# Half of a weight block loaded later, and the last two shuffles of an inverse transform sent by halves on three queues

## The chip, the cores and the metric

The kernel runs on one core of a Trainium2 chip. The metric is the device time of one execution in microseconds. A core has TensorE (matmul), VectorE, ScalarE, GpSimd and SyncE, which run their own instruction streams and wait for each other through semaphores, and 16 DMA engines, which move data on behalf of whichever engine issued the transfer. In the profile these are PE (with PEld for its weight loads), DVE, ACT, POOL and SP.

## The reference

S = 2048 positions, D = 448 channels, a hidden size F = 1792, everything in bf16. With LN a layer norm over D without weights:

```
h   = q + LN(q) * y,   y = causal convolution over S of kv with ssm_k, plus kv * ssm_D
kv  = v * (4-tap causal convolution of k with shift_k)
h2  = h + transpose( gelu( LN(LN(h))^T @ w1 + b1 ) @ w2 + b2 )
```

The long convolution is written as rfft, product, irfft of length 2 S. The MLP mixes positions: w1 is S x F, w2 is F x S.

## The kernel before, in words

The positions are split as s = 16 q + r: q is the partition (128 of them) and r the row (R = 16). A transform of length 4096 is done in two stages of matmuls, with a shuffle of partitions between them, which is a DMA from SBUF to SBUF. So there is a forward stage 1 for the filter and for kv (`emit_stage1`, tables E), its shuffles (L947), a forward stage 2 (`emit_stage2`, L964), and then the way back in `emit_products_i1`: for each of eight pairs jj the complex products on VectorE (L1015), inverse stage 1 on TensorE (L1027), the evacuation of PSUM into the SBUF tile TU (L1031, which is the helper `evac`: its instructions carry lines 652 and 653 on ScalarE and 655 and 656 on VectorE), and the shuffle of TU into the tile TZ (L1037). TU is indexed [partition, j, h, d] with j = 0 to 15 and h = 0, 1 the two halves of a complex number. An evacuation of pair jj writes one h for both j = 2 jj and 2 jj + 1. A shuffle moves one j with both h: 112 partitions of it from GpSimd's queue, 16 partitions from SyncE's.

Inverse stage 2 (`emit_i2`, L1104) is two matmuls for each of the 16 rows. It reads, for every row, all 16 shuffles, so it starts only once the last has landed. Behind it per row come the gate on ScalarE or VectorE (L1111), a combination on VectorE (L1118), the second layer norm (sums on ScalarE L1134, small steps on GpSimd L1141 to L1153, the normalised row Q on VectorE L1159), and, interleaved on TensorE, the first seven blocks of the MLP's first layer (L1203), which use the weights W1A. The other seven blocks (L1213) use W1B, the second layer (L1223) uses W2. The results go out at L1231 and L1234.

Between inverse stages 1 and 2 there are filler matmuls (`emit_warm`, L1047): 34 of them (N_WZ) ahead of stage 2, and 6 and 8 more inside it. They compute nothing that is used. The statistics of q for the first layer norm are on VectorE (L1069, L1071) with two small steps on GpSimd for each group of two rows (L1074, L1077), in whatever gaps there are.

The loads: q into X (L838) and W1A in four parts of four rows each (L1178) wait for the last shuffle of kv (`shuf["upool15"]`). W2 (L1188, four parts) and W1B (L1181, four parts) wait for the last large inverse shuffle (`shuf["zpool"]`). All of them are issued by SyncE (WQ), whose instruction stream is in order, as every engine's is. TK and TU give their space to W2, V and the tables E give theirs to W1B.

The order of instructions isn't written out by hand. `op(...)` records each operation with what it reads and writes, and when all are recorded a planner (`schedule`) walks through simulated time. When an engine comes free, it takes the ready operation with the earliest due time `sch.t0` (the length of the path behind it only breaks near ties), using estimated durations and one shared rate for DMA. `emit` then writes the instructions in the planned order and adds the waits. Due times that matter here: 7.01 + 0.974 i for the inverse products, evacuations and shuffles (i = 15 gives 21.62), T_Q = 83.98 and later for the statistics of q, 35.76 and later for the 34 fillers, 85.76 and later for stage 2, T_W1 = 122.45 for W1A, T_W1 + 4 = 126.45 for W2, T_WB = 154.44 for W1B.

Of the kernel before, what the change touches and what calls it, by code (L numbers as in the profile page):

```python
# [98 lines left out]
class _Sched:  # L99
# [48 lines left out]
    def op(self, W, fn, r=(), w=(), br=(), bw=(), n=0, kind=None, est=None, dmab=None, keng=16, rate=None, after=(), safter=()):  # L148
        o = _Op()
        o.id = len(self.ops)  # L150
        o.engs = W if isinstance(W, tuple) else (W,)
        o.eng = None
        o.fn = fn
        o.is_dma = dmab is not None
        o.nbytes = dmab or 0
        o.keng = keng
        o.lat = 2000.0 + o.nbytes / (22.0 * keng) if o.is_dma else 70.0
        if o.is_dma:
            o.est = {e: (600.0 if e != "pool" else 820.0) for e in o.engs}
        elif est is not None:  # L160
            o.est = dict(est) if isinstance(est, dict) else {e: est for e in o.engs}
        else:
            o.est = {e: self.est_of(e, n, kind) for e in o.engs}
        o.ev = None
        o.t0 = self.t0
        o.rate = rate or (18.0 if keng == 8 else 26.0)
        o.tag = self.tag
        o.acq = []
        o.bufs = []
        o.extra = []  # L170
        preds = set(after)
        spreds = set(safter)
        for spec in r:
            for c in self._cells(spec):
                preds.update(c.w)
                c.r.append(o.id)
        for spec in w:
            g = spec[2] if len(spec) > 2 else None
            for c in self._cells(spec):
                rd = [x for x in c.r if x != o.id]  # L180
                if g is not None and c.g == g and not rd:
                    preds.update(c.gb)
                    c.w.append(o.id)
                else:
                    base = rd if rd else list(c.w)
                    preds.update(base)
                    c.w = [o.id]
                    c.r = []
                    c.g = g
                    c.gb = base  # L190
        for b in br:
            if len(self.ops) and all(self.ops[x].engs == ("pe",) for x in b.writers):
                preds.add(b.writers[-1])
            else:
                preds.update(b.writers)
            b.readers.append(o.id)
            o.bufs.append(b)
            b.users.append(o.id)
        for b in bw:
            if not b.writers:  # L200
                o.acq.append(b)
            else:
                spreds.add(b.writers[-1])
            b.writers.append(o.id)
            o.bufs.append(b)
            b.users.append(o.id)
        preds.discard(o.id)
        spreds -= preds
        o.preds = sorted(preds)
        o.spreds = sorted(spreds)  # L210
        self.ops.append(o)
        return o.id
# [297 lines left out]
def _build(nc, A_q, A_k, A_v, A_shift_k, A_ssm_k, A_ssm_D, B_w1, B_b1, B_w2, B_b2, out):  # L510
# [8 lines left out]
    R = 16  # L519
    NFC = F // 128  # L520
    EPS = 1e-5
    DB = 2 * D
# [15 lines left out]
    o_W1A = 0  # L538
# [8 lines left out]
    o_TU = 104064  # L547
    o_KN = o_TU
    o_W2 = (o_TK, o_TU)
    o_TZ = 132736  # L550
# [15 lines left out]
    with ctx:  # L566
        sch = _Sched(nc, ctx, n_dma_sems=112, small_off=SMALL)
        op = sch.op
# [4 lines left out]
        def view(off, shape, dtype=bf16):  # L573
            size = 4 if dtype in (f32, i32) else 2
            n = 1
            for s_ in shape:
                n *= s_
            ap = AR[:, off // 2: off // 2 + n * size // 2]
            if dtype is not bf16:
                ap = ap.bitcast(dtype)  # L580
            if len(shape) == 2:
                ap = ap.rearrange("p (a b) -> p a b", b=shape[1])
            elif len(shape) == 3:
                ap = ap.rearrange("p (a b c) -> p a b c", b=shape[1], c=shape[2])
            return ap
# [8 lines left out]
        TU = view(o_TU, [R, 2, D])  # L594
        KN = view(o_KN, [4, S])
        W2 = [view(o, [NFC // 2, S]) for o in o_W2]
        TZ = view(o_TZ, [R, 2, D])
# [15 lines left out]
        def MR(s):  # L613
            return view(o_WR + s * 4 * DB, [4, D])
# [13 lines left out]
        def Pb(b, i=0):  # L628
            return PS[:, b.slots[i], 0:D]

        def Ppair(b):
            s0, s1 = b.slots
            return PS[:, s0:s1 + 1, 0:D]
# [7 lines left out]
        T_Q, T_DQ, T_I2, T_DI2, T_M1, T_W1 = 83.98, 14.35, 85.76, 0.401, 102.98, 122.45  # L641

        T_TH, T_TN = -36.0, -30.0
        T_CP, T_XL, T_WB = 20.0, -35.53, 154.44
# [309 lines left out]
        shuf = {}  # L954
# [50 lines left out]
        def emit_products_i1():  # L1005
            for jj in range(R // 2):
                ms = []
                for h in range(2):
                    i = 2 * jj + h
                    sch.t0 = T_I1 + T_DI1 * i  # L1010
                    m = _Buf(mring)
                    ms.append(m)
                    ru = (o_TU + i * 2 * DB, 2 * DB)
                    aft = [x for w in wbufs for x in w.readers] if i == 0 else [mfirst[0]]
                    op("dve", lambda e, W, m=m, i=i: e.tensor_tensor(  # L1015
                        out=MR(m.slots[0]).rearrange("p (x y) d -> p x y d", x=2),
                        in0=TU[:, i].unsqueeze(2).broadcast_to([128, 2, 2, D]),
                        in1=TK[:, i].unsqueeze(1).broadcast_to([128, 2, 2, D]), op=ALU.mult),
                       r=[ru, (o_TK + i * 2 * DB, 2 * DB)], bw=[m], n=4 * D, after=aft)
                    if i == 0:  # L1020
                        mfirst.append(len(sch.ops) - 1)
                bs = [_Buf(psum, 2) for _ in range(2)]
                for h in range(2):
                    for t, (tab, xy) in enumerate(((MA, 0), (MN, 3), (MB, 1), (MB, 2))):
                        for par in range(2):
                            P = slice(64 * par, 64 * par + 64)
                            k = op("pe", lambda e, W, b=bs[h], m=ms[h], par=par, t=t, tab=tab, xy=xy, P=P: e.matmul(  # L1027
                                Pb(b, par), tab[P, :], MR(m.slots[0])[P, xy, :], start=(t == 0), stop=(t == 3)),
                               r=r_iv, br=[ms[h]], bw=[bs[h]], n=D, est=D / 4.15)
                            i1_last.append(k)  # L1030
                    evac(lambda jj=jj, h=h: TU[:, 2 * jj:2 * jj + 2, h, :], lambda b=bs[h]: Ppair(b),  # L1031
                         [(o_TU + (4 * jj + h) * DB, DB), (o_TU + (4 * jj + 2 + h) * DB, DB)], bs[h], 2 * D)
                for par in range(2):
                    j = 2 * jj + par
                    p0 = 64 * (j & 1) + 32 * ((j >> 1) & 1) + (j >> 2)
                    for q_, a, b_, j0 in (("pool", 0, 112, 0), ("sp", 112, 128, 14)):
                        shuf["z" + q_ + str(j)] = shuf["z" + q_] = op(q_, lambda e, W, j=j, p0=p0, a=a, b_=b_, j0=j0: e.dma_start(  # L1037
                            TZ[p0:p0 + 29:4, j0:j0 + (b_ - a) // 8].rearrange("p r c d -> p r (c d)"),
                            TU[a:b_, j].rearrange("p c d -> p (c d)")),
                           r=[(o_TU + j * 2 * DB, 2 * DB)], w=[(o_TZ + j0 * 2 * DB, (b_ - a) // 8 * 2 * DB, "z" + q_)],  # L1040
                           dmab=(b_ - a) * 2 * DB, keng=8)
# [130 lines left out]

        def emit_w1_load(which):
            for h in range(4):
                sch.t0 = (T_W1, T_WB)[which] + 0.1 * h * (1 - which)
                rs = slice(4 * h, 4 * h + 4)
                if which == 0:
                    op(WQ, lambda e, W, rs=rs: e.dma_start(W1A[:, rs, :], w1d[:, rs, 0:896]),  # L1178
                       w=[(o_W1A + 4 * h * 1792, 4 * 1792)], dmab=128 * 4 * 1792, after=[shuf["upool15"]])
                else:  # L1180
                    op(WQ, lambda e, W, rs=rs: e.dma_start(W1B[:, rs, :], w1d[:, rs, 896:1792]),  # L1181
                       w=[(o_W1B + 4 * h * 1792, 4 * 1792)], dmab=128 * 4 * 1792, after=[shuf["zpool"]])
# [100 lines left out]
```

## Time and profile before

| | |
|---|---|
| median of five runs | 189.56 us (188.29 to 191.54) |
| the profiled execution's own time | 189.56 us |
| its span in the profile | 187.7 us |
| TensorE busy | 174.2 us (93%) |
| VectorE, ScalarE, GpSimd busy | 109.9, 97.3, 70.9 us |
| TensorE's granted clock | 1.00 |
| moved by DMA | 35.43 MB, 129 GB/s of HBM traffic over the span |

The 1.86 us between the time and the span lie around the span. The profile has a page with each engine's busy time, groups of instructions by source line, and a chain of waits: followed back from the last instruction, at each step, to what released it. A timeline lists the instructions of an engine in order of time, equal neighbours merged, with the idle time before them and what ended it. A table of windows gives the busy time of every engine in a stretch. A DMA's duration on its issuing engine is only the issue; the landing is counted from the start of the issue to the end of the transfer.

### The profile page before, as it was taken

What the parts mean: (1) busy time and instruction counts of PE and PEld (TensorE: products, weight loads), DVE (VectorE), ACT (ScalarE), POOL (GpSimd) and SP (SyncE); (2) the same over time, 40 slices, a digit from 0 to 9 for tenths busy, and PEclk for the clock granted to TensorE, in tenths of its full rate; (3) what the DMA queues carried; (4) which work ended last, traced back from release to release, by engine and by line L of the source; (5) the groups of instructions that cost most, each with busy time, mean ns of one, the idle gap of its engine ahead of it and who ended that gap; (6) DMA issues with size and microseconds to landing.
All of it is one profiled execution on the core that took longest, in us unless ns stands there. A gap on an engine that the chain in (4) does not pass through costs nothing.

```text
span 187.7 us, 2824 instructions
## 1 busy us (share of the span) xinstructions
PE 174.2 (93%) x1033; PEld 91.6 (49%) x1033; DVE 109.9 (59%) x181; ACT 97.3 (52%) x141; POOL 70.9 (38%) x176
## 2 busy tenths in 40 slices
PE   7998898988988989899989999999999999999993
PEld 2752343423432433244435545555557777777771
DVE  8877999777789999997879756000001122222221
ACT  3597989788789989950986483442121000000000
POOL 8936977678520034577178566000000000000000
PEclk9999999999999999999999999999999999999999
DMA  5997688787449997773999999000000110111111
GB/s 160 413 416 287 187 242 237 213 250 220 119 120 376 391 377 215 226 228 116 320 421 418 419 402 369 10 0 0 0 0 3 49 43 6 49 52 49 49 49 49
DMA packets 15724, 35.43 MB, mean 189 GB/s; under 512 B 3869, under 2 KB 9886, under 8 KB 15710
## 3 DMA queue, kind: packets, MB, share of 16 engines
q1 hardware_dynamic: 11102, 25.59, 36.3%
q0 software_dynamic: 4608, 9.66, 17.8%
q8 instruction: 8, 0.13, 0.3%
q14 instruction: 6, 0.05, 0.1%
HBM read 22.37 MB, written 1.84 MB: 129 GB/s over the span
## 4 chain that ended last, share of the span: by engine, by line
PE 68%; DMA 9%; ACT 8%; DVE 5%; POOL 5%; issue 3%; ACTq 0%; SPq 0%; POOLq 0%
PE ps L1223 23%; PE ps L1213 11%; PE ps L1203 10%; DMA arena<-arena 9%; PE ps L1027 5%; ACT arena L652 4%; PE ps L964 4%; PE ps L1104 3%; POOL arena L947 3%; PE ps L914 3%; PE ps L904 3%; ACT arena L943 2%; PE ps L1047 2%; ACT arena L1111 1%; PE ps L996 1%
## 5 line engine op out<-in xcount | busy, mean ns | idle before, releaser
L1227 DVE SCALAR_TENSOR_TENSOR arena<-ps,arena 128x448 bf16<-128x448 f32 x16 | 10.9, 684 | 56.9 <-PE ps L1223 56.9
L1223 PE MATMUL ps<-arena 128*128 128x448 bf16 x224 | 42.5, 352 | 0.0
L1223 PEld LDWEIGHTS ps<-arena 128*128 128x128 bf16 x224 | 32.3, 144 | 10.1
L943 ACT CAST arena<-ps 128x896 bf16<-128x896 f32 x32 | 26.8, 928 | 4.1 <-PE ps L933 1.5
L652 ACT CAST arena<-ps 128x896 bf16<-128x896 f32 (+1 forms) x26 | 22.0, 909 | 2.6 <-PE ps L868 1.6
L1203 PE MATMUL ps<-arena 128*128 128x448 bf16 x112 | 23.0, 353 | 0.3 <-DVE arena L1159 0.2
L947 POOL DMA_DIRECT2D arena<-arena x32 | 19.2, 601 | 8.5 <-ACT arena L943 5.0
L1213 PE MATMUL ps<-arena 128*128 128x448 bf16 x112 | 21.4, 352 | 0.0
L1193 ACT ACTIVATE arena<-ps,arena 128x448 bf16<-128x448 f32 x14 | 8.2, 639 | 20.1 <-PE ps L1213 14.7
L964 PE MATMUL ps<-arena 128*64 128x448 bf16 x128 | 16.4, 362 | 2.0 <-ACT arena L652 1.0
L879 DVE TENSOR_TENSOR arena<-arena 128x1792 bf16<-128x1792 bf16 x16 | 18.2, 1173 | 0.0
L1111 ACT ACTIVATE arena<-ps,arena 128x448 f32<-128x448 f32 x16 | 11.2, 721 | 12.3 <-PE ps L1104 9.3
L1037 POOL DMA_DIRECT2D arena<-arena x16 | 9.4, 594 | 20.8 <-PE ps L964 15.6
L933 PE MATMUL ps<-arena 128*128 128x448 bf16 x64 | 16.0, 355 | 1.3 <-ACT arena L943 1.3
L885 PE MATMUL ps<-arena 128*128 128x448 bf16 x64 | 14.5, 353 | 2.4 <-ACT arena L943 1.9
L1015 DVE TENSOR_TENSOR arena<-arena 128x1792 bf16<-128x1792 bf16 x16 | 16.4, 1084 | 0.0
L1203 PEld LDWEIGHTS ps<-arena 128*128 128x128 bf16 x112 | 10.9, 98 | 11.1 <-DVE arena L1159 1.3
L1213 PEld LDWEIGHTS ps<-arena 128*128 128x128 bf16 x112 | 11.0, 98 | 10.2
L1027 PE MATMUL ps<-arena 64*128 64x448 bf16 x128 | 14.1, 351 | 1.3 <-DVE arena L1015 0.6
L1118 DVE SCALAR_TENSOR_TENSOR arena<-arena 128x448 f32<-128x448 bf16 x16 | 10.7, 676 | 4.8 <-ACT arena L1111 4.8
L964 PEld LDWEIGHTS ps<-arena 128*64 128x64 f16 x128 | 5.4, 108 | 11.7 <-ACT arena L652 4.6
L655 DVE CAST arena<-ps 128x896 bf16<-128x896 f32 (+2 forms) x11 | 9.5, 877 | 2.7 <-PE ps L868 1.2
(87 smaller groups left out, 197.9 us busy)
## 6 DMA issues: line engine op xcount, KB each, us to landing
arena<-arena POOLq DMA_DIRECT2D x48, 196.0 KB, 4.9
arena<-in_B_w_dram SPq DMA_DIRECT2D x8, 896.0 KB, 12.9
arena<-in_B_w_dram SPq DMA_DIRECT2D x2, 2048.0 KB, 10.4
arena<-in_B_w_dram SPq DMA_DIRECT2D x2, 1536.0 KB, 17.5
arena<-in_A_k_dram SPq DMA_DIRECT2D x4, 448.0 KB, 7.4
arena<-in_A_v_dram SPq DMA_DIRECT2D x4, 448.0 KB, 8.0
arena<-in_A_q_dram SPq DMA_DIRECT2D x4, 448.0 KB, 4.6
out_dram<-arena SPq DMA_DIRECT2D x7, 224.0 KB, 1.9
```

What stands on the lines that cost most here:

```text
L652: return e.copy(out=dst(), in_=src())
L879: op("dve", lambda e, W, T=T, i=i, r=r: e.tensor_tensor(out=T[:, i], in0=KH[:, r:r + 4, :], in1=WT, op=ALU.mult), r=[(o_KH + r * DB, 4 * D ...
L885: op("pe", lambda e, W, b=b, T=T, i=i, j=j: e.matmul(Pb(b, i), ID, T[:, i, j, :], start=(j == 0), stop=(j == 3)), r=[(o_ID, 256), (o + (i ...
L933: op("pe", lambda e, W, b=b, r=r, h=h, dl=dl: e.matmul(Pb(b, h), E[:, 2 * r + h, :], src[:, r, :], start=True, stop=not dl), r=[r_E(r), (o ...
L943: return e.copy(out=dst, in_=Ppair(b)) if W == "act" else e.tensor_copy(out=dst, in_=Ppair(b))
L947: shuf[tag + q_ + str(r)] = shuf[tag + q_] = op(q_, lambda e, W, w=w, p0=p0, a=a, b_=b_, j0=j0: e.dma_start(T[p0:p0 + 29:4, j0:j0 + (b_ - ...
L964: op("pe", lambda e, W, b=bs[h], h=h, j=j, c=c, par=par: e.matmul(PS[64 * par:64 * par + 64, b.slots[c], 0:D], FW[:, 64 * c:64 * c + 64], ...
L1015: op("dve", lambda e, W, m=m, i=i: e.tensor_tensor(out=MR(m.slots[0]).rearrange("p (x y) d -> p x y d", x=2), in0=TU[:, i].unsqueeze(2).br ...
L1027: k = op("pe", lambda e, W, b=bs[h], m=ms[h], par=par, t=t, tab=tab, xy=xy, P=P: e.matmul(Pb(b, par), tab[P, :], MR(m.slots[0])[P, xy, :], ...
L1203: op("pe", lambda e, W, r=r, fc=fc, b=bs[fc]: e.matmul(Pb(b), W1A[:, r, 128 * fc:128 * fc + 128], Q[:, r, :], start=(r == 0), stop=(r == R ...
L1213: op("pe", lambda e, W, r=r, fc=fc, b=b: e.matmul(Pb(b), W1B[:, r, 128 * (fc - n0):128 * (fc - n0) + 128], Q[:, r, :], start=(r == 0), sto ...
L1223: op("pe", lambda e, W, r=r, fc=fc, b=b: e.matmul(Pb(b), W2[fc // 7][:, fc % 7, r:S:R], G[:, fc, :], start=(fc == 0), stop=(fc == NFC - 1) ...
```

## The change

The change has two parts.

First, for the last pair of inverse shuffles (jj = 7, j = 14 and 15) the two h are sent apart, so that each transfer depends on one evacuation only. The h = 0 halves go as before: 112 partitions from GpSimd, 16 from SyncE. Of the h = 1 halves, the 112 partitions of j = 14 go from GpSimd and those of j = 15 from SyncE, and both times the 16 remaining partitions from ScalarE's queue. `shuf["zpool"]` is then the transfer of j = 15, h = 1 on SyncE.

Second, parts 2 and 3 of W1A (rows 8 to 15) wait for `zpool` instead of `upool15`, with a due time 30 earlier (92.45). W1B's due time is 30 earlier as well (124.44), which puts it ahead of W2 (126.45).

```diff
@@ emit_products_i1, in the loop over jj, ahead of the shuffles
+                if jj == R // 2 - 1:
+                    for h in range(2):
+                        for par in range(2):
+                            j = 2 * jj + par
+                            p0 = 64 * (j & 1) + 32 * ((j >> 1) & 1) + (j >> 2)
+                            o_h = o_TU + (2 * j + h) * DB
+                            for q_, a, b_, j0 in (("sp" if h and par else "pool", 0, 112, 0), ("act" if h else "sp", 112, 128, 14)):
+                                k = op(q_, lambda e, W, j=j, h=h, p0=p0, a=a, b_=b_, j0=j0: e.dma_start(
+                                    TZ[p0:p0 + 29:4, j0:j0 + (b_ - a) // 8, h, :], TU[a:b_, j, h, :]),
+                                       r=[(o_h, DB)], w=[(o_TZ + j0 * 2 * DB, (b_ - a) // 8 * 2 * DB, "zpool" if a == 0 else "zsp")],
+                                       dmab=(b_ - a) * DB, keng=8)
+                                if a == 0:
+                                    shuf["zpool"] = k
+                    continue
@@ emit_w1_load
-                sch.t0 = (T_W1, T_WB)[which] + 0.1 * h * (1 - which)
+                sch.t0 = (T_W1 - 30.0 * (h > 1), T_WB - 30.0)[which] + 0.1 * h * (1 - which)
...
-                       w=[(o_W1A + 4 * h * 1792, 4 * 1792)], dmab=128 * 4 * 1792, after=[shuf["upool15"]])
+                       w=[(o_W1A + 4 * h * 1792, 4 * 1792)], dmab=128 * 4 * 1792,
+                       after=[shuf["upool15" if h < 2 else "zpool"]])
```

## The prediction

> **What bounds the kernel now.** I read the chain of waits first, then the timeline of TensorE, GpSimd and ScalarE around the place that the change touches, then the windows of the stages behind it. The chain, in order of time (start us, us, what), from the last inverse products on:
>
> ```profile
> 79.59 0.91 ACT arena L652
> 80.50 0.28 issue
> 80.79 1.17 POOL arena L1037 x2
> 81.95 0.07 issue
> 82.03 0.24 POOL arena L1074
> ...
> 82.35 0.72 POOL arena L1077
> 83.07 0.64 POOL arena L1037
> 83.71 4.62 DMA arena<-arena
> 88.33 0.05 issue
> 88.37 1.70 PE ps L1104 x8
> ```
>
> So the last shuffle of TU into TZ (L1037) starts at 83.71, lands at 88.33, and the inverse stage 2 (L1104) starts at 88.37. It reads as if every microsecond off that shuffle were a microsecond off the kernel. TensorE's timeline (start, busy us, line, count, idle before) says otherwise:
>
> ```profile
> 81.62 6.60 PE L1047 MATMUL ps<-arena 128*128 128x448 f16 x34
> 88.37 1.69 PE L1104 MATMUL ps<-arena 128*128 128x448 bf16 x8
> ```
>
> The 34 filler matmuls of L1047 stand in TensorE's program ahead of L1104. A matmul lasts 352 ns and overlaps the next, so 6.60 us = 33 steps + 0.352, a step of 0.189 us. The last filler starts at 81.62 + 6.25 = 87.87 and the next matmul could start at 88.06. TensorE therefore waits for the shuffle for only 88.37 - 88.06 = 0.31 us. The weight loads say the same within their own lead: 0.59 us idle, put down to the DMA.
>
> Behind that point TensorE is the bound (us, then busy time and count of PE, PEld, DVE, ACT, POOL; clock; DMA share; GB/s):
>
> ```profile
> 88.37:112.80 24.43, 23.21 (x116) 10.46 (x116) 18.60 (x56) 17.86 (x40) 14.25 (x37) 1.00 0.97 383
> 112.80:120.94 8.14, 8.12 (x43) 4.22 (x44) 2.86 (x7) 2.50 (x8) 3.04 (x8) 1.00 0.55 209
> 120.94:142.13 21.19, 21.19 (x114) 11.05 (x112) 0.00 (x0) 6.49 (x12) 0.00 (x0) 1.00 0.00 0
> ```
>
> From 88.37 to the end there are about 1.2 us in which TensorE does not work. All else is a fixed count of matmuls, 14 more fillers among them, at a granted clock of 1.00.
>
> **The last pair of shuffles.** Before, j = 14 and 15 need both evacuations of the pair, and are 2 issues on GpSimd (587 to 674 ns) and 2 small ones on SyncE (0.67 us). GpSimd:
>
> ```profile
> 80.79 1.17 POOL L1037 DMA_DIRECT2D arena<-arena  x2 [0.84 <-ACT arena L652]
> 82.03 0.24 POOL L1074 TENSOR_SCALAR arena<-arena 128x2 f32<-128x2 f32 x1
> 82.35 0.72 POOL L1077 TENSOR_TENSOR arena<-arena 128x2 f32<-128x2 f32 x1
> 83.03 1.27 POOL L1037 DMA_DIRECT2D arena<-arena  x2
> ```
>
> ScalarE's timeline has the two last evacuations back to back:
>
> ```profile
> 80.65 1.85 ACT L652 CAST arena<-ps 128x896 bf16<-128x896 f32 x2 [0.15 <-PE ps L1027]
> 88.96 2.57 ACT L1111 ACTIVATE arena<-ps,arena 128x448 f32<-128x448 f32 x4 [6.46 <-PE ps L1104]
> ```
>
> so half h = 0 is ready at about 81.57 and h = 1 at 82.50. After, there are 8 issues: 3 on GpSimd, 3 on SyncE, 2 on ScalarE. GpSimd is free at 81.96; its two h = 0 halves take it to 81.98 + 2 x 0.59 = 83.16, and the third (j = 14, h = 1) starts there: 0.55 us before the last one of now. The statistics steps L1074/L1077 fall behind all three, because their due time (83.98) is later than the shuffles' (21.62) and the planner now has a shuffle ready for each free slot. SyncE is free at 81.9 (its jj = 6 issues began at 80.52 and take 0.67 each); two small ones, then the large j = 15, h = 1 starts at 81.93 + 2 x 0.67 = 83.27. ScalarE issues its two small ones from 82.53.
>
> Landings. On GpSimd the shuffles of this stage land 3.7 to 6.0 us after issue starts, median 4.8; the last took 4.62. Half the bytes in the same number of rows: at best 3.7, at worst 6.0; I take the last one's own 4.62, giving 83.16 + 4.62 = 87.78. The Trainium skill (DMA: Bandwidth & Descriptors, section Anatomy of one DMA — SWDGE (gpsimd) path) puts a transfer at a fixed part of about 2.0 us plus bytes over 436 GB/s. By it halving 196 KB saves an estimated 0.23 us, and a half is through some 2.2 us after its 0.59 us issue, at 86.0. The trace is twice as slow, and I use the trace; the sum is the same by both, since both fall ahead of 88.06. The same page (section Issuing engines are not separate DMA queues) speaks against the split: more issuing engines save only issue time, because all run on the same 16 DMA engines. By that rule the gain is the 0.55 us of issue above, not a shorter flight.
>
> No SyncE shuffle of this size stands in the trace. Nearest below are its output stores, 112 KB in 1.7 us; nearest above its X loads, 448 KB in 3.6 to 5.8 us under a full DMA. I take 3.7, the fastest GpSimd shuffle, since it too is SBUF to SBUF: 87.0, with ends 85.0 and 89.1. A DMA from ScalarE is not in the trace at all. Its issue is bounded by 0.59 (GpSimd's) and 1.30 us (SyncE's longest at L1037), an addition, so no gain; I take 0.67 each. They hide in ScalarE's 6.46 us idle before L1111 at 88.96, which is what is queued behind them; with that cover gone they would cost 1.3 us. Their landing has the bounds of the SyncE ones, and a first use of a queue gives a third row: SyncE's very first load, 256 KB, landed in 3.7. From 83.2 that is 86.9. What a third queue costs outside the span lies between 0 and 0.9 us (two queues and everything else fit in 189.56 - 187.7 = 1.86); no row separates it out, so I take 0 and keep the end for the range.
>
> So all of TZ is there at about 87.8, and L1104 starts at 88.06 instead of 88.37: **-0.31 us**. The other 0.28 us of earlier landing goes into the fillers. Next to be late is TensorE itself. Four more semaphore waits ahead of L1104 count as nothing: after the last landing all the remaining ones took 0.04 us.
>
> **GpSimd behind it.** One more issue (0.59) pushes the last statistics step before stage 2 from 88.03 to 88.6. The gate of row 0 needs only the first step, done at about 84.8; rows 8 and 9 need the last one at 97. GpSimd's next other work is at 92.47. Nothing.
>
> **The moved loads.** Two of four W1A loads (2 x 896 KB) leave the stretch 56 to 70. There the DMA is full (share 1.05 at 64 to 68), but the chain from 55 to 80 has no DMA in it, and shuffles issued under that load land in 4.4 to 5.1 us, not later than those after it. Gain: nothing. They reappear behind the SyncE half, ahead of W1B and W2, with the due times putting W1B before W2. Before, W2 and W1B are 10752 KB = 11.0 MB, at 413 GB/s 26.7 us, from about 90.3 to 117. After, SyncE resumes at about 87.0, data flows from about 89, and the half W1A takes 1.84 MB / 413 = 4.4 us, to 93.5; W1B 8.9 us, to 102.4; W2 17.8 us, to 120. Add 1 us for completion. Needs: W1A's row 8 is matmul 57 of L1203, the sixth of the seven that start at 107.61, hence 108.6; W1B at 120.94; W2 at 142.13. Margins 14, 17 and 21 us. If the old order W2 before W1B had been kept, W1B would land at 121 and its first matmul wait; it isn't. SyncE has no other work until the stores at 148.18. Starting these loads while the last GpSimd half is in flight costs nothing by the row just quoted.
>
> **The order.** The planner is list scheduling over the whole program, so an edit may reorder far away. By its own costs the fillers (34 at 190 ns, from the last product on) end 0.1 us after the last shuffle already before, so stage 2 starts at the same planned time in both, and the loads needed later are there long before. I expect the same order on TensorE, VectorE and ScalarE.
>
> Sum against the profiled execution: span 187.7 - 0.31 = 187.4; time 189.56 - 0.31 = 189.25. That execution's time equals the median of the runs, so **189.3**.
>
> **Rivals.** (a) *The landing sets the start.* If the planner put fewer fillers ahead of L1104, or the halves' short landing pulled more than 0.31 us: landing at 87.0 to 87.8 gives 0.6 to 1.4 us, 188.2 to 189.0. For it: the chain names the shuffle. Against it: the fillers' count, and TensorE's 1.2 us of idle behind, which caps even a better order. Chance 0.07.
> (b) *Slower: the last quarter lands late.* Place: ScalarE's second small shuffle, begun at 83.2, or SyncE's large one, begun at 83.27, ahead of L1104. It decides from a landing of 88.33, that is 5.1 us of flight; each microsecond beyond is one lost. At the slowest flight in this stage, 6.0 us, it lands at 89.3: +0.9, 190.5. For it: rows of 896 B instead of 1792 B, and a queue never used in the trace. Against: 3.7 for a first use. Chance 0.10.
> (c) *It doesn't do what it says.* L1074 and L1077 (1.04 us with gaps) still fall ahead of the last GpSimd half, as they do now: start 84.2, landing 88.8, +0.45: 190.0. For it: they do so in the profile. Against: the due times. Chance 0.05.
>
> **How the numbers follow.** The forecast, 189.3, has 0.78. The five runs spread from 188.29 to 191.54, and about 1% is what a measurement of this kernel can tell from no change. The range reaches down to rival (a) and up past (b): 188.3 to 190.7. Faster by over 1% needs 1.9 us, more than the idle that is there: 0.05. Slower by over 1% needs a flight of 7 us or a reordered stage 2: 0.10. Within 1%: 0.85.
>
> **What would show it.** Right: the fillers still x34 and ending near 88.2, L1104 starting at about 88.1 with no wait for the DMA, three GpSimd issues in a row before L1074, W1A's halves landing before 95, no wait for a load in L1203 or L1213. Wrong: L1104 still waiting for a DMA beyond 88.4; another interleaving of L1104, L1047 and L1203; matmuls of L1203 waiting on a load near 108.

## The result, and the profile after

The changed kernel takes 190.11 us (median of 43 executions, 187.83 to 193.31) beside 189.84 us for the kernel before (80 executions, 187.40 to 192.70). The ratio is 1.0025, with a 95% interval from 1.0006 to 1.0044: slower by about 0.5 us, with 0.1 and 0.8 as the ends. That ratio counts only executions within 1.5% of the fastest of their own kernel; over all of them the means differ by 0.38 us, with an interval from -0.1 to 0.9 (95%, by resampling the listed times). So how much slower it is, and whether it is at all, is less sure than the first interval looks, but a gain of 0.31 us, which was the forecast, lies outside both. The time itself lies inside the range and within the 1% that was called no change, but the sign was wrong.

The profiled execution of the changed kernel has a span of 186.9 us, 0.8 less than the one of before, and that says nothing about the change. Its fillers start at 80.90 instead of 81.62, because loads and shuffles ahead of 50 us, which the change doesn't touch, happened to come earlier. So the stretches have to be compared one by one. The chain of the changed kernel (start us, us, what) around the place of the change:

```profile
80.87 0.91 ACT arena L652
81.79 0.14 SPq L1040
81.92 0.04 issue
81.97 1.33 SPq L1040
83.30 0.04 issue
83.34 4.49 DMA arena<-arena
87.83 0.09 issue
87.92 1.69 PE ps L1118 x8
```

Before, the last piece ahead of stage 2 was GpSimd's second shuffle (4.62 us from 83.71). Now it is a SyncE one, the large half of j = 15, which starts 1.56 us behind the last evacuation (83.34 against 81.78) and flies 4.49 us. SyncE goes on with W1A at 87.85, which confirms the landing, since that load waits for this half. TensorE's timeline:

```profile
80.90 6.61 PE L1061 MATMUL ps<-arena 128*128 128x448 f16 x34
87.92 1.67 PE L1118 MATMUL ps<-arena 128*128 128x448 bf16 x8 [0.42 <-DMA arena<-arena]
```

From the first filler to stage 2 it is 7.02 us, against 6.75 before and 6.44 if nothing but the 34 fillers counted. The wait for the DMA did not go; between these two profiles it grew by 0.27 us. GpSimd and ScalarE did what the prediction had written down for them, apart from ScalarE's two issues, which took 1.96 us instead of 1.34:

```profile
81.22 1.75 POOL L1040 DMA_DIRECT2D arena<-arena  x3
83.05 0.42 POOL L1088 TENSOR_SCALAR arena<-arena 128x2 f32<-128x2 f32 x2
...
81.81 1.96 ACTq L1040 DMA_DIRECT2D arena<-arena  x2
```

Behind stage 2 the two profiles agree window by window (columns as in the prediction):

```profile
87.92:112.36 24.44, 23.20 (x117) 10.45 (x117) 18.63 (x56) 17.89 (x40) 14.26 (x37) 1.00 0.99 377
112.36:120.48 8.12, 8.12 (x43) 4.22 (x44) 2.83 (x7) 2.48 (x8) 3.03 (x7) 1.00 1.03 418
120.48:141.67 21.19, 21.19 (x113) 11.05 (x112) 0.00 (x0) 6.48 (x12) 0.00 (x0) 1.00 0.04 15
```

These are 24.44, 8.12 and 21.19 us against 24.43, 8.14 and 21.19. The DMA is full some 4 us longer (share 1.03 in the second window instead of 0.55), and TensorE doesn't notice.

### The profile page after: what moved, and what is told of

It is laid out like the page before. It is cut to its first block, busy times and chain, and to the rows that moved or that the text cites. A ratio compares the mean times of both kernels' runs of the same rounds, so it can differ in the third digit from the quotient of the medians.

```text
span 186.9 us, 2835 instructions
## 1 busy us (share of the span) xinstructions
PE 174.2 (93%) x1033; PEld 91.6 (49%) x1033; DVE 110.0 (59%) x181; ACT 97.1 (52%) x141; POOL 72.1 (39%) x177
## 4 chain that ended last, share of the span: by engine, by line
PE 72%; DMA 10%; ACT 8%; DVE 6%; issue 2%; SPq 1%; ACTq 0%
PE ps L1238 23%; PE ps L1228 11%; PE ps L1218 10%; DMA arena<-arena 7%; PE ps L885 5%; PE ps L1027 5%; ACT arena L652 4%; PE ps L964 4%; PE ps L1118 3%; PE ps L933 3%; DMA arena<-in_A_ssm_k_dram 3%; DVE arena L1015 2%; PE ps L914 2%; ACT arena L943 2%; PE ps L1061 2%
## 5 line engine op out<-in xcount | busy, mean ns | idle before, releaser
L1218 PE MATMUL ps<-arena 128*128 128x448 bf16 x112 | 23.0, 353 | 0.3 <-DVE arena L1173 0.2
L947 POOL DMA_DIRECT2D arena<-arena x32 | 19.2, 601 | 6.5 <-ACT arena L943 3.5
L1228 PE MATMUL ps<-arena 128*128 128x448 bf16 x112 | 21.4, 352 | 0.0
L964 PE MATMUL ps<-arena 128*64 128x448 bf16 x128 | 16.4, 362 | 1.8 <-ACT arena L652 1.0
L1218 PEld LDWEIGHTS ps<-arena 128*128 128x128 bf16 x112 | 10.9, 98 | 11.1 <-DVE arena L1173 1.3
L1051 POOL DMA_DIRECT2D arena<-arena x14 | 8.2, 588 | 20.8 <-PE ps L964 15.6
L1228 PEld LDWEIGHTS ps<-arena 128*128 128x128 bf16 x112 | 11.0, 98 | 10.2
L964 PEld LDWEIGHTS ps<-arena 128*64 128x64 f16 x128 | 5.4, 108 | 11.4 <-ACT arena L652 4.6
```

What stands on the lines that cost most here:

```text
L947: shuf[tag + q_ + str(r)] = shuf[tag + q_] = op(q_, lambda e, W, w=w, p0=p0, a=a, b_=b_, j0=j0: e.dma_start(T[p0:p0 + 29:4, j0:j0 + (b_ - ...
L964: op("pe", lambda e, W, b=bs[h], h=h, j=j, c=c, par=par: e.matmul(PS[64 * par:64 * par + 64, b.slots[c], 0:D], FW[:, 64 * c:64 * c + 64], ...
L1218: op("pe", lambda e, W, r=r, fc=fc, b=bs[fc]: e.matmul(Pb(b), W1A[:, r, 128 * fc:128 * fc + 128], Q[:, r, :], start=(r == 0), stop=(r == R ...
L1228: op("pe", lambda e, W, r=r, fc=fc, b=b: e.matmul(Pb(b), W1B[:, r, 128 * (fc - n0):128 * (fc - n0) + 128], Q[:, r, :], start=(r == 0), sto ...
```

## The experiments

The times of whole executions scatter by 1 to 2% for causes ahead of the change, so the main measure is the stretch F, from the start of the first filler to the start of stage 2. From stage 2 to the end of the last VectorE instruction it was 96.83 to 96.86 us in every profile at full clock in that stretch, of every kernel below. F is therefore where the kernels differ behind the fillers.

| kernel | F in each profile, us | time against before, 95% interval |
|---|---|---|
| before | 6.75, 7.04, 6.91 | |
| changed | 7.02, 6.99, 7.20 | 1.0025 (1.0006 to 1.0044) |
| shuffles only | 7.12 | 1.0009 (0.9976 to 1.0042) |
| loads only | 6.44, 6.53, 7.09 | 0.9997 (0.9946 to 1.0049) |
| changed, small ones on SyncE | 7.18 | 1.0017 (0.9969 to 1.0065) |
| changed, all large halves on GpSimd | 6.66, 6.62, 6.70 | 1.0108 (1.0048 to 1.0168), then 0.9990 (0.9955 to 1.0026) |
| the same without the moved loads | 7.16 | 0.9966 (0.9934 to 0.9997) |
| whole rows from ScalarE and SyncE | 6.69 (at a clock of 0.94), 7.98 | 1.0004 (0.9972 to 1.0036) |
| loads only, statistics behind, 31 fillers | 6.87 | 0.9971 (0.9940 to 1.0002) |
| before, one shuffle more | 7.76 | |
| before, half the bytes in the last pair | 6.44 | |

### One part at a time

The first part alone is the changed kernel with the load function of before; the second alone is the kernel before with

```diff
-                sch.t0 = (T_W1, T_WB)[which] + 0.1 * h * (1 - which)
+                sch.t0 = (T_W1 - 30.0 * (h > 1), T_WB - 30.0)[which] + 0.1 * h * (1 - which)
...
-                       after=[shuf["upool15"]])
+                       after=[shuf["upool15" if h < 2 else "zpool"]])
```

> The first part of the change alone: the last pair of shuffles by halves on three queues; all of W1A waits for the kv shuffles and W2 goes before W1B, as before. Measure: from the start of the first of the 34 fillers to the start of inverse stage 2, which is 6.75 us before and 7.02 after the change, with 6.44 the floor that the fillers set. Theory (the SyncE half of j = 15 starts late, because the ScalarE and SyncE issues slow each other, and flies long): 7.0 us, the same as with the whole change, and a time 0.2 to 0.4 us above before. Rival (the moved loads cost it): 6.75 or less, and no slower than before.

> The second part alone: half of W1A and all of W1B wait behind the last shuffle, W2 last; the shuffles as before. Theory (late SyncE half): fillers to stage 2 stay at 6.75 us, from stage 2 to the end 96.2 us as in both profiles, time within 0.2% of before. Rival (the loads cost it): a longer stretch behind stage 2, or 7.0 us ahead of it, and a time 0.2 to 0.4% above before.

Shuffles only: F = 7.12, as with the whole change. Loads only: no wait at all in the first profile.

```profile
80.31 6.61 PE L1047 MATMUL ps<-arena 128*128 128x448 f16 x34
86.75 1.49 PE L1104 MATMUL ps<-arena 128*128 128x448 bf16 x7
```

So the lateness seems to come with the split, not with the loads, on one profile each. The times are too blunt to say it: both intervals hold 1. What was not expected is that F fell to the floor with the loads moved. The stretch was profiled twice more.

> The moved loads alone, once more, for a second profile. If moving W1A out of the stretch before really speeds the last shuffle, stage 2 is at the floor of 6.44 us behind the first filler again. If the 6.44 was one draw of a scattering landing, it is 6.7 to 7.0 as in the profiles of before.

> The moved loads alone, a third profile. If moving half of W1A speeds the last shuffle, 6.44 to 6.6 us from the first filler to stage 2; if the two low ones were chance, 6.75 or more.

It gave 6.53 and then 7.09, with a wait again:

```profile
83.21 6.61 PE L1047 MATMUL ps<-arena 128*128 128x448 f16 x34
90.30 0.55 PE L1104 MATMUL ps<-arena 128*128 128x448 bf16 x2 [0.48 <-DMA arena<-arena]
```

Whether the moved loads help the landing stays open on these three. Behind stage 2 they cost nothing, as the unchanged stretch shows.

### How much F scatters

The kernel before and the changed one were run unchanged.

> The kernel before, unchanged, for a second profile of the same stretch. If the stretch from the first of the 34 fillers to stage 2 is a property of the kernel, it is 6.75 us again, within 0.1; if landings of the last shuffle scatter, it can be anything from the floor of 6.44 to 6.9.

> The changed kernel, unchanged, for a second profile. Theory (the hardware-queue half of j = 15 lands last): 6.9 to 7.2 us again, and the shuffle that lands last is SyncE's, since SyncE goes on with W1A in the same tenth of a microsecond as stage 2 starts. Rival (scatter): below 6.75.

> The kernel before, a third profile. From the first filler to stage 2 it had 6.75 and 7.04. If it belongs between the moved loads alone (6.44, 6.53) and the changed kernel (7.02, 6.99, 7.20), it has 6.7 to 7.05 again. If all three are one scatter, it can be 6.44 or 7.2.

> The changed kernel, a third profile. 7.0 us from the first filler to stage 2 again if the lateness is the kernel's; scatter would show as 6.7 or less.

Before has 6.75, 7.04, 6.91 (mean 6.90), changed 7.02, 6.99, 7.20 (mean 7.07). The second profile of before:

```profile
83.35 6.61 PE L1047 MATMUL ps<-arena 128*128 128x448 f16 x34
90.39 0.55 PE L1104 MATMUL ps<-arena 128*128 128x448 bf16 x2 [0.43 <-DMA arena<-arena]
```

The landing scatters by some 0.3 us in the same program. The wait of 0.31 us that the prediction was built on was one draw; over three profiles it is 6.90 - 6.44 = 0.46. The means differ by 0.17 us, which lies inside the measured 0.1 to 0.8 us, but the two sets overlap: 7.04 of before is above 7.02 and 6.99 of the changed kernel. Where the rest of the middle value (0.47) would be was not found, and with these scatters it need not exist.

### ScalarE's issues, taken away

```diff
-("act" if h else "sp", 112, 128, 14)
+("sp", 112, 128, 14)
```

> The whole change, but the two small h = 1 shuffles go from SyncE's queue behind its large one, and ScalarE issues none. Theory (the issues of ScalarE and SyncE slow each other): SyncE's second small issue takes 0.7 us instead of 1.33, its large half starts 0.6 us earlier and lands 0.5 us earlier, at some 6.4 to 6.6 us behind the first filler; stage 2 starts at 6.45 to 6.6 us, time 0.3 to 0.5 us below that of the whole change. Rival (flight alone is long, the engines' bandwidth ends it): the large half still lands at about 6.9 us, stage 2 at 7.0.

F = 7.18, as the rival had it. SyncE's issues were no quicker without ScalarE beside them. The five of this kernel took up to 1.15 us, and one ahead of them 1.45, so the collision of the two engines' issues is not needed to explain slow ones. The large half began 2.4 us behind the last evacuation, later than in the changed kernel, and still landed at nearly the same time (6.2 us behind it, against 6.0 to 6.2). That was the first sign that the start of the issue is not what sets the landing.

### The large half back on GpSimd

```diff
-(("sp" if h and par else "pool", 0, 112, 0), ...
+(("pool", 0, 112, 0), ...
```

> The whole change, but the large h = 1 half of j = 15 goes from GpSimd as well, which then issues four halves in a row; SyncE and ScalarE have the small ones alone. Theory (the half on the hardware queue is late because its 112 rows of 896 B come up one packet at a time beside GpSimd's packets of three to five rows): the last GpSimd half starts 0.6 us later than now, at some 2.1 us behind the first filler, flies 4.2 to 5.0 us and lands at 6.3 to 7.0; stage 2 at 6.4 to 7.0 us, earlier than with the whole change by 0.1 to 0.5. Rival (halving the rows is what makes flights long, on any queue): 7.1 us or more.

> The whole change with all four large halves of the last pair on GpSimd, once more. If it is SyncE's half that makes the changed kernel late, 6.5 to 6.8 us (6.66 in the first profile); if halving alone makes it late, 7.0 or more.

> The whole change with all four large halves of the last pair on GpSimd, a third time, now with a time over more executions (the first time rested on four). In its two profiles stage 2 started 6.66 and 6.62 us behind the first filler, against 6.75 to 7.04 before. Theory (that stretch is all that differs between the kernels, the rest of the spread comes from ahead of it): 6.6 to 6.7 us again and a time 0.1 to 0.5 us below before. Rival (the 1.1% slower of the first time is the kernel's): slower than before by over 0.5% again.

> The same halves on GpSimd, but W1A, W1B and W2 as before the change. Theory (the halves bring it, the loads are neutral): 6.55 to 6.75 us from the first filler to stage 2, time 0.1 to 0.5 us below before. Rival (the moved loads bring it): 6.75 to 7.05, no faster than before.

With the loads moved F is 6.66, 6.62 and 6.70, all below all of the changed kernel's, though GpSimd now has four issues one behind the other:

```profile
81.40 2.33 POOL L1040 DMA_DIRECT2D arena<-arena  x4
```

```profile
81.07 6.61 PE L1061 MATMUL ps<-arena 128*128 128x448 f16 x34
87.69 0.55 PE L1118 MATMUL ps<-arena 128*128 128x448 bf16 x2
```

The first is GpSimd's timeline, the second TensorE's, of the second profile. TensorE reports no wait here. F is 0.24 us below the mean of before and 0.41 below that of the changed kernel. So with the loads moved, one queue name is worth 0.4 us. The landings agree: in all five profiles with this half on SyncE (changed, shuffles only, small ones on SyncE) the trace's semaphore records have it 0.2 to 0.5 us behind GpSimd's last half.

With the loads as before, the same two versions, with the half on SyncE (shuffles only) and on GpSimd, were equal in their one profile each:

```profile
81.10 6.60 PE L1061 MATMUL ps<-arena 128*128 128x448 f16 x34
88.22 1.67 PE L1118 MATMUL ps<-arena 128*128 128x448 bf16 x8 [0.52 <-issue]
...
81.57 6.61 PE L1061 MATMUL ps<-arena 128*128 128x448 f16 x34
88.73 1.69 PE L1118 MATMUL ps<-arena 128*128 128x448 bf16 x8 [0.55 <-DMA arena<-arena]
```

F is 7.12 and 7.16, both above all three of before. So either the queue counts only together with the moved loads, or the 7.16 is one high draw. That halving is late on any queue while the loads stand as before is a rival that these runs leave standing.

The times of these kernels show how blunt they are. The same program gave 1.0108 on four executions and 0.9990 on fourteen, with intervals that don't touch. The first lot took 191.1 to 191.7 us, and in its profile the fillers start at 83.91, in the next one at 81.07. The same caution holds for the 1.0025 of the changed kernel. None of these versions can be called faster than before by its time. The interval of the no-loads version (0.9966) just leaves 1 out, but its own F is longer than that of before.

### Both last ones from the hardware queues, whole rows

The kernel before with the large part of j = 14 on ScalarE, of j = 15 on SyncE. The profile calls these two engines' queues hardware queues and GpSimd's a software queue.

> The kernel before with two transfers of the last pair on other queues: the large part of j = 14 (whole rows, both h) from ScalarE, the large part of j = 15 from SyncE, then the two small ones from SyncE; GpSimd issues none for this pair. Theory (issue starts and flights of 4.5 us set the landing): both large ones start within 0.1 to 0.8 us of the last evacuation, the landing is at 5.6 to 6.2 us behind the first filler, so the fillers hide it: stage 2 at 6.44 us, no wait for a DMA, time 0.3 us below before. Rival (shuffles from these queues fly longer than GpSimd's): landing past 6.75 us, stage 2 at 6.8 to 7.5 us, slower than before.

> The kernel before with the large parts of j = 14 and 15 whole from ScalarE and SyncE, once more, for a profile at full clock. If the two hardware queues serve whole rows well when GpSimd sends nothing for this pair, stage 2 starts at 6.44 to 6.7 us behind the first filler; if those queues are slow by themselves, 7.0 or more.

The first profile has a granted clock of 0.94 over the execution, its fillers take 6.85 us, and stage 2 follows them at 6.69; by the semaphore records the two large ones land 5.1 and 5.5 us behind the last evacuation. The second, at full clock:

```profile
82.36 0.02 issue
82.38 6.80 DMA arena<-arena
89.17 0.28 issue
89.45 1.69 PE ps L1104 x8
```

This is the chain. Both large ones start at 82.38, 0.03 us behind the last evacuation, earlier than any other version's last shuffle. The semaphore records have SyncE's landing at 89.17 and ScalarE's at 89.36, 7.0 us after its start. F = 7.98. A shuffle from these queues can start early and still land last. The two profiles disagree by 1.5 us and more on the landing, so what sets it is not shown.

The same records have SyncE's two small shuffles landing at 89.55 and 89.73, behind the start of stage 2 at 89.45. They fill only rows 14 and 15 of TZ (`j0 = 14`), which are planned last. So what stage 2 needs for its start is the large shuffles alone.

### More and less in the DMA engines

One more transfer of 196 KB in the kernel before, issued by SyncE between the last two pairs, into free space:

```diff
+                if jj == R // 2 - 1:
+                    PX = view(o_PR, [R, 2, D])
+                    op("sp", lambda e, W: e.dma_start(PX[0:29:4, 0:14].rearrange("p r c d -> p r (c d)"),
+                                                      TU[0:112, 12].rearrange("p c d -> p (c d)")), ...)
```

> The kernel before, with one more large shuffle of whole rows (196 KB, j = 12 once more, into unused space) that SyncE issues between the last two pairs. Nothing but the weight block W1B waits for it. Measure: from the end of the last evacuation to the landing of the last GpSimd shuffle, 5.8 to 6.1 us in the two profiles of before. Theory (the DMA engines' backlog sets the landing, not the issue): 196 KB more at the 225 to 290 GB/s that this stage moves is 0.7 to 0.9 us, so 6.4 to 7.0 us, and stage 2 at 7.3 to 7.9 us behind the first filler. Rival (a flight is a fixed time behind its issue): 5.8 to 6.1 us as before, since GpSimd's issues stay where they are.

The chain of this kernel:

```profile
87.17 0.64 POOL arena L1042
87.80 5.62 DMA arena<-arena
93.42 0.05 issue
93.46 1.12 PE ps L1109 x5
```

GpSimd's last issue still starts 1.22 us behind the last evacuation (86.58), as in before. Its flight is 5.62 instead of 4.62 us, F is 7.76, and the landing is 6.84 us behind the evacuation. So a transfer that nobody on the path waits for moved the landing by 0.7 to 1.0 us (it was at 5.8 to 6.1 in before). On this one profile, what is queued ahead counts, not the start of the issue alone.

The other way round, the last pair moved only its h = 0 half.

```diff
-                            TZ[p0:p0 + 29:4, ...].rearrange("p r c d -> p r (c d)"), TU[a:b_, j]...
+                            ... if j < 14 else TZ[p0:p0 + 29:4, j0:j0 + (b_ - a) // 8, 0, :], TU[a:b_, j, 0, :]
```

> The kernel before, but of the last pair (j = 14 and 15) only the h = 0 half is moved at its place, in the same four issues; the place of the h = 1 halves is filled some 12 us earlier from j = 0, so that part of the inverse transform works on wrong data. Theory (backlog): 224 KB less behind the last evacuation, 0.8 us: landing 4.6 to 5.3 us behind it, and stage 2 held by the fillers at 6.44. Rival (a fixed flight): at most the 0.2 us that half the bytes take at full rate, 5.5 to 5.9 us.

F is at the floor, and the landing is 5.48 us behind the evacuation (SyncE's next load starts at 87.62, the evacuation ended at 82.14), against 5.84 to 6.13 in before. The last flights were 4.3 and 4.7 us. That lies between the two expectations, next to the rival's 5.5: half the bytes seem to save 0.4 to 0.6 us, not 0.8. But loads only landed 5.42 us behind its last evacuation in one profile with all the bytes, so one profile does not tell this saving from scatter.

### An earlier start on GpSimd

Loads only, with the statistics steps placed behind the last two shuffles in GpSimd's program, and three fillers left out.

```diff
+        mv = [x for x in order[:zl] if self.ops[x].tag == "q" and self.ops[x].eng == "pool" and self.start_t[x] > t_z - 3000.0]
+        order = [x for x in order[:zl + 1] if x not in mv] + mv + order[zl + 1:]
...
+            if oid in warm[31:]:
+                continue
```

> The moved loads alone, with the last pair's shuffles as before, but in GpSimd's program the statistics steps that stood ahead of the last two shuffles stand behind them, and 31 of the 34 fillers ahead of stage 2 remain (the order of all else as in the moved loads alone). Theory (issue starts set the landing): GpSimd starts the last pair 0.1 us instead of 0.5 us behind the last evacuation and it lands 0.4 us earlier, at 5.8 to 6.3 us behind the first filler; the floor is 31 steps of 0.189, 5.87; stage 2 at 5.9 to 6.3 us, time 0.4 to 0.8 us below before. Rival (the DMA engines' backlog sets the landing whenever the issue starts): landing at 6.3 to 6.7, time within 0.2% of before.

```profile
82.93 6.04 PE L1055 MATMUL ps<-arena 128*128 128x448 f16 x31
89.80 0.55 PE L1112 MATMUL ps<-arena 128*128 128x448 bf16 x2 [0.83 <-DMA arena<-arena]
```

GpSimd's last issue began 0.87 instead of 1.21 us behind the last evacuation, but the landing was 5.96 us behind it, as in before. Thus F = 6.87, and the fillers that were left out became waiting. The theory missed here; the rival was nearer, and even its 6.7 was passed, at 6.82 behind the first filler.

## Why the prediction was right and wrong

**Right: the bound.** 34 fillers, and behind them a TensorE that nothing else holds up. The floor of 6.44 us was reached in two kernels, and the rest of the path kept its 96.83 to 96.86 us.

**Right: the loads.** No row of L1218 or L1228 waits for a load in the changed kernel. The second half of W1A was issued at 87.85 and 88.3 and landed 4.8 and 7.2 us later, by 95.5 (96.2 in the times of before), against a forecast of 94.5 and a need at 108.6. W1B and W2 came in that order with wide margins.

**Right: the order of the programs.** TensorE's interleaving of L1118, L1061 and L1218 is that of before, and GpSimd's three issues stand ahead of the statistics steps. Rival (c) fell. The third queue cost nothing outside the span: time less span is 188.73 - 186.9 = 1.8 us, as before.

**Wrong: the landing of SyncE's half.** The step that failed is the forecast that this half would start at 83.27 and land at 87.0. Moved to the times of before (0.72 later than in this profile), it started at 84.06 and landed at 88.55. Two terms were short, by 0.79 us each: the start, mostly as SyncE's second small issue took 1.33 us instead of 0.67, and the flight, 4.49 us instead of 3.7. Either one alone would have left the landing at about 87.76, ahead of the 88.06 at which the fillers end; together they passed it. In the other two profiles the start was 0.4 and 0.6 us later than forecast and the flight some 4.85 us. What repeats is the landing, 6.0 to 6.2 us behind the last evacuation, where the forecast had 4.5 (87.0 against 82.5). The semaphore waits that were put at nothing took another 0.04 us: from the landing to stage 2 it was 0.09 us instead of 0.05. GpSimd's own last half was off in the same direction: 5.0 us of flight instead of 4.62, a landing at 88.1 instead of 87.78.

Behind both stands one idea that the runs speak against: that a flight is a size of its own that follows the start of its issue. A GpSimd start 0.34 us earlier left the landing where it was (statistics behind); a foreign transfer lengthened the flight by 0.7 to 1.0 us (one shuffle more); a half of 98 KB flew 5.0 us where a whole of 196 KB had flown 4.6 to 4.9. Over every version with the full traffic and a full clock, the landing was 5.4 to 6.2 us behind the last evacuation, apart from the 6.8 and 7.0 of the whole rows on the hardware queues.

Rival (b) named the right transfer, SyncE's large half, and the right point, a landing at 88.33; ScalarE's small one, which it named beside it, could not hold up the start of stage 2, which does without the small ones (see the whole rows above). It was given a chance of 0.10, because the shortest flight of a GpSimd shuffle, 3.7 us, stood for a SyncE one. The median of the same shuffles, 4.8 us, would have put the landing at 88.07, with no slack left against 88.06.

**The rule that speaks against the split** held more strictly than it was read. The Trainium skill (DMA: Bandwidth & Descriptors, section Issuing engines are not separate DMA queues) says that more issuing engines save only issue time. Here GpSimd's last start came 0.6 us earlier behind the last evacuation (0.61 instead of 1.21), its landing only by 0.2 us on the mean (5.6 to 5.8 instead of 5.8 to 6.1), and SyncE's half, at 6.0 to 6.2, took even that away. The other figure that the prediction took from the page (section Anatomy of one DMA — SWDGE (gpsimd) path), 2.0 us and bytes over 436 GB/s, gives an estimated 2.2 us for a half; the large halves of the changed kernel's profile took 4.5 to 5.4.

**Open.** Why a half on SyncE lands later than the same half on GpSimd was not shown. The trace has two candidates. GpSimd's queue moves the shuffles in packets of 3584 to 5376 B, the hardware queues in packets of one row, 896 or 1792 B; in the changed kernel the last 112 half rows on SyncE's queue run from 85.69 to 87.23, most of them once GpSimd's packets, which end at 86.70, thin out. And as its data land, a GpSimd shuffle raises its semaphore 16 times, as a weight load on SyncE does, but a shuffle on SyncE or ScalarE only 8 times. That suggests, without proving it, that these shuffles use half of the 16 DMA engines. No run separated either from other causes. Nor is it settled whether the moved loads help: with whole rows on GpSimd two of three profiles say so, with halves on GpSimd all three against the single one without them.

## What to carry to other kernels

If the chain names a transfer, measure how long the waiting engine could have been held by its own program anyway, and profile the kernel more than once before a few tenths of a microsecond are built on: here the wait was 0.31, 0.60 and 0.47 us in the same program. Where the DMA is busy with the same kind of traffic (a share of 0.74 from 79 to 86 us before), don't count on a split over more queues to bring the last transfer in earlier: here it did not, and the traffic queued ahead, and with the loads moved the choice of the queue, made more difference than the start of the issue. An issue that starts earlier is not a landing that comes earlier.

## What was not expected of the hardware

SyncE's issues of small shuffles mostly take 0.67 us, but up to 1.45 us in the kernel where no other engine issues on a hardware queue. The time to the first filler differed by 2.5 us between the three profiles of the kernel before (80.81 to 83.35 us). This makes most of the spread of 1 to 2% in the times. Between the first two profiles it is there by 52 us, where the chain reaches L964 (50.46 and 52.20 us).
